# Attention with a Fourier mix and MLP: state products between the key and query turns, output turns behind the outputs, fixed PSUM banks, 17 unread products at the start

## The chip, the cores and the metric

The kernel runs on one core of one Trainium2 chip. The metric is the device time of an execution in microseconds; lower is better. A profile shows one execution: TensorE (PE, and PEld for its weight loads), VectorE (DVE), ScalarE (ACT), GpSimd (POOL) and the DMA queues, which SyncE (SP), ScalarE and GpSimd issue.

## The reference

```python
# batch 4, heads 8, seq 768, head_dim 64; blocks of 64 in the sequence
for b in range(nb):
    intra = einsum('bhic,bhjc->bhij', qb, kb) * Dmask      # lam**(i-j), lower triangle
    intra = einsum('bhij,bhjd->bhid', intra, vb)
    inter = einsum('bhid,bhde->bhie', qb * lam_pow, kv_state)
    out[:, :, sl] = intra + inter
    kv_state = lam_block * kv_state + einsum('bhsd,bhse->bhde', kb * rev_pow, vb)
# heads joined: x is (4, 768, 512)
mixed = real(fft(fft(x, axis=1), axis=2))
u = x + mixed
un = (u - mean(u)) / sqrt(var(u) + 1e-6)                   # over the 512 columns
out = u + maximum(un @ w_ch1, 0) @ w_ch2                   # 512 -> 2048 -> 512, weights come as float64
```

## The kernel before

All of it is float32. The attention works in chunks of 128 rows; a step `i` of twelve handles two chunks of one batch (three steps, `n = 0, 1, 2`, to a batch) for all eight heads, on 64x64 pieces of the array. A step has these parts, each a function:

- `turn_k` and `turn_q` turn keys and queries over by TensorE (eight 128x128 transposes each); ScalarE copies them from PSUM to `kT` and `qT` (lines 395, 401), and VectorE multiplies the queries by powers of lambda to `qs` (line 403);
- `scores` multiplies keys by queries into four PSUM banks (line 429), from which VectorE copies, times the decay, to `sc` (line 435, four instructions);
- `from_state` multiplies `qs` by the states of the chunks before (line 444), `within` the scores by v on top of that (line 450); ScalarE copies the result out as `oT`, in batch 0 also mirrored as `oTs` (lines 456 to 466);
- `to_state` multiplies scaled keys by v (line 409); VectorE adds it to a state (lines 417, 419) and GpSimd multiplies a state by its decay (`decayed`, line 424). `scale` scales the keys on GpSimd (line 389), after a small copy `scored` that waits for the first of VectorE's score copies; `sort` puts the keys of a later step in order (line 383);
- `back` turns the outputs over (`turned`, line 470) and copies them to rows, right half reversed (`put`, lines 480 and 481).

`attention` is a generator that calls these in an order written by hand, and every engine keeps that order. Where it yields, units of other work are put in: `w` is a third of a weight piece's conversion from float64 (`convert`: DVE and ScalarE, lines 264 to 273), `m` a step of the Fourier transform and normalisation of batch 0 (`fft_ln`, lines 601 to 839), `l` and `k` hidden-layer products (`mlp`, line 921). The lists `PLAN` (for each step a triple, one string for each yield) and `REST` (behind the attention) say how many. Behind them, from about 190 us on, a scheduler orders the rest by itself.

PSUM has eight banks, printed as `pa_96` to `pa_100` (banks 0 to 4) and `pm_101` to `pm_103` (banks 5 to 7). Turns, scores, output turns and at times state products draw in turn from banks 0 to 3 (`psum_t`), outputs from 4 and 5, Fourier products and most state products from 6 and 7 (`psum_a`).

Of the kernel before, what the change touches and what calls it, by code (L numbers as in the profile page):

```python
# [77 lines left out]
def kernel(  # L78
# [14 lines left out]
    C = 128  # L93
# [62 lines left out]
    turn = {"s": 0, "m": 0, "o": 0}  # L156
# [8 lines left out]
    def psum_t(shape):  # L165
        turn["s"] += 1
        return held_bank((turn["s"] - 1) % 4, shape)

    def psum_o(shape):
        turn["o"] += 1  # L170
        return held_bank(4 + (turn["o"] - 1) % 2, shape)
# [16 lines left out]
    make_identity(nc, ident)  # L188
    scan = nc.vector.tensor_tensor_scan
# [164 lines left out]
    po = {}  # L354
    mm = nc.tensor.matmul
# [35 lines left out]
    def turn_k(i):  # L391
        for r in range(2):
            pt = psum_t([128, HP, 128])
            lead(P(nc.tensor.transpose(pt[:, hp, :], k2[:, r, 128 * hp:128 * hp + 128], ident)) for hp in range(HP))  # L394
            P(nc.scalar.copy(kT[:, r], pt))

    def turn_q(i):
        for ch in range(2):
            pt = psum_t([128, HP, C])
# [5 lines left out]
    def to_state(i):  # L405
        n, vt, kd = i % SC, v_of[i % 2], k_of[i % 2]
        chunks = (0, 1) if n < SC - 1 else (0,)
        pu = [(psum_t if unread[0] or i < 2 else psum_a)([128, HP, D]) for _ in chunks]
# [3 lines left out]
        with tc.high_priority(100):  # L412
            for ch in chunks:
                c = 2 * n + ch
                s_new = states[(c + 1) % 3]
                if c == 0:
                    P(nc.vector.tensor_copy(s_new, pu[ch]))
# [9 lines left out]
    def scores(i):  # L427
        pss = [[psum_t([128, HP, C]) for _ in range(2)] for _ in range(2)]
# [11 lines left out]
    def from_state(i):  # L440
        n = i % SC
        po[i] = [psum_o([128, HP, C]) for _ in range(2)]
# [5 lines left out]
    def within(i):  # L448
# [4 lines left out]
        o = oT[i] = new(at, [128, HP, 2 * C], "oT")  # L453
        if b not in TURNED:
            for ch in range(2):
                P(nc.scalar.copy(o[:, :, C * ch:C * ch + C], po[i][ch]))
            return
        z = oTs[i] = new(at, [128, HP, 2 * C], "oTs", bufs=2)
        P(nc.scalar.copy(o[:, :, 0:C], po[i][0]))
        P(nc.scalar.copy(first if n == 0 else oTs[i - 1][:, :, 0:1], po[i][0][:, :, 0:1]))  # L460
        P(nc.scalar.copy(z[:, :, 2 * C - 1:C:-1], po[i][0][:, :, 1:C]))
        P(nc.scalar.copy(z[:, :, C:0:-1], po[i][1]))
        if n < SC - 1:
            P(nc.scalar.copy(o[:, :, C:2 * C], po[i][1]))
        else:
            P(nc.scalar.copy(z[:, :, 0:1], first))

    def turned(o, cols):
        px = psum_t([C, HP, 128])
# [3 lines left out]
    def put(px, x, n=128, crossed=False):  # L473
# [6 lines left out]
        P(nc.scalar.copy(x[0:n, 0:HM], px[0:n, 0:HM]))  # L480
        P(nc.scalar.copy(x[0:n, HM:DM], px[0:n, DM - 1:HM - 1:-1]))
# [1158 lines left out]
```

## Time and profile before

| | |
|---|---|
| median of 3 runs | 779.84 us (778.29 to 783.93) |
| the profiled execution | 780.86 us, its span 779.1 us |
| TensorE busy | 744.9 us (96%), 6872 instructions |
| VectorE busy | 604.6 us (78%) |
| ScalarE / GpSimd busy | 208.5 / 195.0 us |
| mean granted TensorE clock | 0.995 |

A line of the profile names the source line, the engine, the operation and `out<-in` with buffer numbers left out: `pa<-ident,w` is a transpose into a bank of the pool `pa`, whose source lies in a tile `w...`. TensorE's matmuls are pipelined and their ends are modelled, so its busy share says how seldom it has nothing in flight, not that it runs at its peak. A wait is put down to what came last; "issue" is time in which the engine waited for nothing that the profile shows.

### The profile page before, as it was taken

To read this page: it belongs to the slowest core of one execution; us is meant where nothing else is said; L and a number is where in the kernel's file an instruction comes from. 1 tells how busy PE (TensorE), PEld (TensorE's weight loads), DVE (VectorE), ACT (ScalarE), POOL (GpSimd) and SP (SyncE) were. 2 spreads that over 40 slices of the span, in tenths; PEclk is the share of its full clock that TensorE was granted. 3 is DMA by queue.
4 is the path that set the end of the run, shared out by engine and by line. 5 is a ranking of instruction groups with operands and counts; after the bars stand their busy time and mean duration, and the time that the engine had idled before them with its cause. 6 is when DMAs were issued, how large, how long until landed. Compare 5 with 4: busy or idle time off the path is not lost.

```text
span 779.1 us, 17084 instructions
## 1 busy us (share of the span) xinstructions
PE 744.9 (96%) x6872; PEld 644.2 (83%) x6872; DVE 604.6 (78%) x1163; ACT 208.5 (27%) x488; POOL 195.0 (25%) x221
## 2 busy tenths in 40 slices
PE   6998998799999989999999999999999999999997
PEld 5887887685486668659847889999999999999997
DVE  4578866668999788465965999689986699758984
ACT  2454545543141111002101221024311342024310
POOL 3344342210013214201104951260015000230013
PEclk9999999999999999999999999999999999999999
DMA  9879876535353447521341374775645455455452
GB/s 214 226 200 234 226 222 177 183 115 162 94 171 121 102 125 213 128 88 48 68 129 54 142 237 139 269 241 191 182 143 157 142 177 178 133 178 177 140 145 69
DMA packets 132740, 123.50 MB, mean 159 GB/s; under 512 B 67006, under 2 KB 93246, under 8 KB 132662
## 3 DMA queue, kind: packets, MB, share of 16 engines
q1 hardware_dynamic: 126902, 103.66, 46.6%
q0 software_dynamic: 4032, 12.99, 4.9%
q10 hardware_dynamic: 1728, 5.77, 2.3%
q8 instruction: 54, 0.88, 0.5%
q14 instruction: 24, 0.20, 0.1%
HBM read 90.66 MB, written 31.73 MB: 157 GB/s over the span
## 4 chain that ended last, share of the span: by engine, by line
PE 73%; DVE 9%; issue 7%; DMA 5%; POOL 3%; ACT 1%; SPq 0%; DVEq 0%; POOLq 0%; ACTq 0%
PE p L1370 21%; PE p L1296 17%; PE pm L935 7%; PE pm L921 7%; PE p L1203 5%; PE pa L921 2%; PE pa L429 2%; PE pa L727 2%; DMA words<-in_k_dram 1%; PE pa L450 1%; PE pa L400 1%; POOL fo L615 1%; PE pa L394 1%; PE pa L470 1%; DMA x<-xb,ix 1%
## 5 line engine op out<-in xcount | busy, mean ns | idle before, releaser
L935 PE MATMUL pm<-w,hr 128*128 128x512 f32 x240 | 106.5, 596 | 0.2 <-DVE w L273 0.2
L921 PE MATMUL pm<-ut,w 128*128 128x256 f32 x416 | 97.1, 386 | 3.3 <-ACT hr L929 2.4
L921 PEld LDWEIGHTS pm<-ut,w 128*128 128x128 f32 x416 | 78.4, 192 | 19.2 <-ACT hr L929 4.4
L935 PEld LDWEIGHTS pm<-w,hr 128*128 128x128 f32 x240 | 45.4, 191 | 51.7 <-issue 49.5
L1391 POOL TENSOR_TENSOR y<-y,u 128x512 f32<-128x512 f32 x12 | 19.9, 1660 | 186.8 <-DVE y L1400 155.5
L1370 PE MATMUL p<-tx,sx 128*128 128x128 f32 x400 | 52.7, 275 | 0.0
L1370 PEld LDWEIGHTS p<-tx,sx 128*128 128x128 f32 x400 | 48.6, 192 | 0.0
L1305 DVE TENSOR_TENSOR ha<-p,ha 128x512 f32<-128x512 f32 x60 | 40.0, 683 | 8.0 <-PE p L1296 7.9
L1376 ACT COPY y<-p 128x128 f32<-128x128 f32 x48 | 12.8, 266 | 103.6 <-PE p L1370 103.1
L1378 DVE TENSOR_TENSOR y<-p,y 128x128 f32<-128x128 f32 x92 | 25.4, 283 | 16.1 <-PE p L1370 9.4
L1370 PE MATMUL p<-w,ha 128*128 128x128 f32 x288 | 37.4, 275 | 0.0
L1305 DVE TENSOR_TENSOR hs<-p,hs 128x512 f32<-128x512 f32 x39 | 26.1, 683 | 12.7 <-PE p L1296 12.7
L929 ACT ACTIVATE hr<-pm 128x256 f32<-128x256 f32 x32 | 12.3, 383 | 86.8 <-PE pm L921 85.1
L1370 PEld LDWEIGHTS p<-w,ha 128*128 128x128 f32 x288 | 34.9, 192 | 0.1
L1296 PE MATMUL p<-sx,tx 128*128 128x128 f32 x264 | 33.9, 275 | 0.0
L429 PE MATMUL pa<-w 64*64 64x128 f32 x768 | 28.4, 284 | 5.2 <-issue 5.1
L615 POOL DMA_INDIRECT fo<-xa,ix x6 | 13.1, 2186 | 75.6 <-PE pa L727 69.9
L1296 PEld LDWEIGHTS p<-sx,tx 128*128 128x128 f32 x264 | 31.6, 192 | 0.0
L265 ACT ACTIVATE e<-e,cvt 128x512 uint16<-128x512 uint16 x32 | 22.9, 720 | 32.4 <-DVE e L264 32.2
L429 PEld LDWEIGHTS pa<-w 64*64 64x64 f32 x768 | 24.5, 140 | 7.8 <-issue 5.9
L910 POOL DMA_INDIRECT out_dram<-y,ix x12 | 13.7, 1143 | 66.5 <-DVE y L970 54.7
L1296 PE MATMUL p<-ur,w 128*128 128x128 f32 x216 | 28.0, 275 | 0.0
(338 smaller groups left out, 1926.5 us busy)
## 6 DMA issues: line engine op xcount, KB each, us to landing
tx<-td SPq DMA_DIRECT2D x84, 256.0 KB, 3.1
tx<-sd SPq DMA_DIRECT2D x63, 256.0 KB, 2.9
words<-in_moe_w_ch_dram SPq DMA_DIRECT2D x23, 512.0 KB, 3.4
w<-in_v_dram SPq DMA_DIRECT2D x12, 512.0 KB, 5.3
words<-in_k_dram SPq DMA_DIRECT2D x11, 512.0 KB
td<-tx SPq DMA_DIRECT2D x21, 256.0 KB, 2.0
raw<-in_moe_w_ch_dram ACTq DMA_DIRECT2D x9, 512.0 KB, 9.1
ud<-x SPq DMA_DIRECT2D x16, 256.0 KB, 2.4
```

The source lines that it names most:

```text
L265: P(nc.scalar.activation(pw, pw, AF.Relu, bias=cvt[:, 0:1], scale=8.0))
L429: lead(P(mm(pss[r][hi][HD[ch], hp, :], lhsT=kT[HD[hi], r, hp, D * ch:D * ch + D], rhs=qT[HD[hi], hp, C * ch:C * ch + C], start=True, stop= ...
L615: P(gather(out=eo[b][a][1][0:n, 1, 0:DM], out_offset=None, in_=xa[:, :], in_offset=row_of(a, n)))
L727: mm = P(nc.tensor.matmul(ps[:, n, :], lhsT=piece(a, i, n), rhs=cs[0:rows, a, i in (2, 3), n, :], start=(a == 0), stop=(a == 1)))
L921: P(nc.tensor.matmul(ps, lhsT=w1[:, c, 128 * fc:128 * fc + 128], rhs=ut[:, c, :], start=(c == 0), stop=(c == KO - 1)))
L935: return P(nc.tensor.matmul(ps, lhsT=hr[(fc - f0) // 4][:, fc % 4, 128 * i:128 * i + 128], rhs=w2[:, fc, :], start=(fc == f0), stop=(fc == ...
L1203: nc.tensor.matmul(ps, lhsT=s2.A[a][:, kt, 128 * i:128 * i + 128], rhs=U[b][:, kt, :], start=(first and kt == 0), stop=(kt == 1), skip_gro ...
L1296: nc.tensor.matmul(ps[:, 128 * i:128 * i + 128], lhsT=ab[m][0][:, 128 * i:128 * i + 128], rhs=ab[m][1], start=(start and i == 0), stop=Tru ...
L1305: V.tensor_tensor(o, p, o, op=ADD)
L1370: nc.tensor.matmul(ps[:, 0:HM // 2], lhsT=ab[m][0][i], rhs=ab[m][1][:, i, :], start=(start and i == 0), stop=(i == HF // 2 - 1), skip_grou ...
L1378: V.tensor_tensor(o, ps[:, 0:HM // 2], o, op=ADD)
L1391: nc.gpsimd.tensor_tensor(o, y, u, op=ADD)
```

## The change

The order in a step is now key turn, state products, sort, query turn, within, output turns, scores, from-state; it was key turn, query turn, output turns, state products, sort, within, scores, from-state. The banks have fixed roles: turns take 0 and 1, scores 0 to 3, outputs 4 and 5, and state products and output turns 6 and 7 with the Fourier products (2 and 3 while a Fourier product stands unread in PSUM). In batch 0 ScalarE copies outputs once, and `mirror` has VectorE make the mirrored tile from that copy, one step later. `put` is done by VectorE for even chunks of batch 0 and two mirrored ones, and the first state of a batch is copied by ScalarE. At the start 17 products of the identity matrix with itself, which nothing reads, stand ahead of the first turn. The normalisation of batch 0 is split in `scaled` and `turned_u`, with a tile of its own for each half. `PLAN` and `REST` are new: 18 units `w` instead of 19 in the attention, 38 instead of 41 in all, 48 `m` instead of 52 in the attention, and two `l` at its end.

```diff
+    for _ in range(17):
+        P(nc.tensor.matmul(banks[7][:, 0:128], lhsT=ident, rhs=ident, start=True, stop=True))
-    def psum_t(shape):
-        turn["s"] += 1
-        return held_bank((turn["s"] - 1) % 4, shape)
+    def spare_bank(shape):
+        if unread[0]:
+            turn["s"] += 1
+            return held_bank(2 + turn["s"] % 2, shape)
+        return psum_a(shape)
...
     def turn_k(i):
         for r in range(2):
-            pt = psum_t([128, HP, 128])
+            pt = held_bank(r, [128, HP, 128])
     def turn_q(i):
         for ch in range(2):
-            pt = psum_t([128, HP, C])
+            pt = held_bank(ch, [128, HP, C])
     def to_state(i):
-        pu = [(psum_t if unread[0] or i < 2 else psum_a)([128, HP, D]) for _ in chunks]
+        pu = [spare_bank([128, HP, D]) for _ in chunks]
...
                 if c == 0:
-                    P(nc.vector.tensor_copy(s_new, pu[ch]))
+                    P(nc.scalar.copy(s_new, pu[ch]))
     def scores(i):
-        pss = [[psum_t([128, HP, C]) for _ in range(2)] for _ in range(2)]
+        pss = [[held_bank(2 * r + hi, [128, HP, C]) for hi in range(2)] for r in range(2)]
...
+        for ch in range(2):
+            P(nc.scalar.copy(o[:, :, C * ch:C * ch + C], po[i][ch]))
+    def mirror(i):
+        if i // SC not in TURNED:
             return
+        n, o = i % SC, oT[i]
         z = oTs[i] = new(at, [128, HP, 2 * C], "oTs", bufs=2)
-        P(nc.scalar.copy(o[:, :, 0:C], po[i][0]))
-        P(nc.scalar.copy(first if n == 0 else oTs[i - 1][:, :, 0:1], po[i][0][:, :, 0:1]))
-        P(nc.scalar.copy(z[:, :, 2 * C - 1:C:-1], po[i][0][:, :, 1:C]))
-        P(nc.scalar.copy(z[:, :, C:0:-1], po[i][1]))
-        if n < SC - 1:
-            P(nc.scalar.copy(o[:, :, C:2 * C], po[i][1]))
-        else:
-            P(nc.scalar.copy(z[:, :, 0:1], first))
+        P(nc.vector.tensor_copy(first if n == 0 else oTs[i - 1][:, :, 0:1], o[:, :, 0:1]))
+        P(nc.vector.tensor_copy(z[:, :, 2 * C - 1:0:-1], o[:, :, 1:2 * C]))
+        if n == SC - 1:
+            P(nc.vector.tensor_copy(z[:, :, 0:1], first))
     def turned(o, cols):
-        px = psum_t([C, HP, 128])
+        px = spare_bank([C, HP, 128])
...
         for i in range(n):
+            if i:
+                mirror(i - 1)
             yield 3.0
             if i + 1 < n:
                 turn_k(i + 1)
-                turn_q(i + 1)
-            yield 2.0
-            if i:
-                back(i - 1)
+                to_state(i + 1)
+                if i + 2 < n:
+                    sort(i + 2)
+            yield 1.0
             if i + 1 < n:
-                to_state(i + 1)
-            if i + 2 < n:
-                sort(i + 2)
+                turn_q(i + 1)
             within(i)
...
-            yield 4.0
+            yield 5.0
+            if i:
+                back(i - 1)
             if i + 1 < n:
                 begin(i + 1)
...
-    REST = "lmwlmwlmwlmwwmkmwkmwkwwkwwlmwlmwlmwlwkmwkwkwkwwww"
+    REST = "wwwlwwwlmlmlmmmmlwlwmmkmkmkwkmmwkwwkwmmkwwwkwwww"
```

TensorE's queue in the step that prepares step 5 (batch 1): before, the two turns, the output turn and the state products stand in this order ahead of the products within the block.

```order
L394 MATMUL pa_98<-ident,w_147 128x128 x4
L394 MATMUL pa_99<-ident,w_147 128x128 x4
L400 MATMUL pa_96<-ident,w_147 128x128 x4
L400 MATMUL pa_97<-ident,w_147 128x128 x4
L470 MATMUL pa_98<-ident,oT_912 128x128 x4
L470 MATMUL pa_99<-ident,oT_912 128x128 x4
L409 MATMUL pm_102<-w_147,words_149 64x64 x16
L450 MATMUL pa_100<-w_146,w_147 64x128
```

The same place after the change (key turn now line 396, state products 411, query turn 402, within 452):

```order
L396 MATMUL pa_96<-ident,w_164 128x128 x4
L396 MATMUL pa_97<-ident,w_164 128x128 x4
L411 MATMUL pm_102<-w_164,words_166 64x64 x16
L402 MATMUL pa_96<-ident,w_164 128x128 x4
L402 MATMUL pa_97<-ident,w_164 128x128 x4
L452 MATMUL pa_100<-w_163,w_164 64x128
```

The state products moved ahead of the query turn, both turns share banks 0 and 1, and the output turn has gone behind the products within the block.

ScalarE's queue at the end of step 0 and the start of step 1, before: five output copies, three weight loads, an activation of a weight piece, then the key copies.

```order
L459 COPY oT_368<-pa_100 128x4x128
L460 COPY first<-pa_100 128x4
L461 COPY oTs_369<-pa_100 128x4x127
L462 COPY oTs_369<-pm_101 128x4x128
L464 COPY oT_368<-pm_101 128x4x128
L251 DMA raw_434<-in_moe_w_ch_dram 128x1024
L251 DMA raw_436<-in_moe_w_ch_dram 128x1024
L251 DMA raw_438<-in_moe_w_ch_dram 128x1024
L265 ACTIVATE e_440<-e_440,cvt 128x512
L395 COPY w_146<-pa_96 128x512
```

The same place after the change:

```order
L457 COPY oT_171<-pa_100 128x4x128
L457 COPY oT_171<-pm_101 128x4x128
L252 DMA raw_451<-in_moe_w_ch_dram 128x1024
L252 DMA raw_453<-in_moe_w_ch_dram 128x1024
L252 DMA raw_455<-in_moe_w_ch_dram 128x1024
L266 ACTIVATE e_457<-e_457,cvt 128x512
L397 COPY w_163<-pa_96 128x512
```

Three copies have left ScalarE, and the activation still stands ahead of the key copies.

TensorE's queue behind the last products within the block, before: the last output turn, hidden-layer products (921) and a turn of normalised rows (794).

```order
L450 MATMUL pm_101<-sc_153,w_147 64x128
L470 MATMUL pa_97<-ident,oT_2306 128x128 x4
L470 MATMUL pa_98<-ident,oT_2306 128x128 x4
L921 MATMUL pa_96<-ut_2082,w_146 128x256 x4
L921 MATMUL pa_97<-ut_2082,w_146 128x256 x4
L794 MATMUL pa_98<-ident,un_2337 128x128 x4
```

After (472 output turn, 864 turn of normalised rows, 741 to 746 a Fourier product, 939 hidden-layer products):

```order
L452 MATMUL pm_101<-sc_170,w_164 64x128
L864 MATMUL pm_103<-ident,e_2206 128x128 x4
L741 MATMUL pa_100<-dt,ys_175 128x128
...
L746 MATMUL pa_100<-dt,ys_176 128x128
L939 MATMUL pm_102<-ut_2202,w_163 128x256 x4
L939 MATMUL pm_103<-ut_2202,w_163 128x256 x4
L472 MATMUL pm_102<-ident,oT_171 128x128 x4
L472 MATMUL pm_103<-ident,oT_171 128x128 x4
```

Other products now stand between the last products within the block and the first of the remaining output turns.

More of the change, by code (lines that the diff above doesn't have):

```diff
@@ L354 @@
     po = {}
+    o_of = [new(at, [128, HP, 2 * C], "oT"), new(up, [128, KO, G * 128], "ut")]
     mm = nc.tensor.matmul
@@ L441, in from_state @@
         n = i % SC
-        po[i] = [psum_o([128, HP, C]) for _ in range(2)]
+        po[i] = [held_bank(4 + ch, [128, HP, C]) for ch in range(2)]
         chunks = (0, 1) if n else (1,)
@@ L492, in back @@
                     px = turned(oT[i], cols)
[L493 to L497 removed]
+                    put(px, x, copy=nc.vector.tensor_copy if ch == 0 else None)
                 continue
@@ L851, in one, with scaled, turned_u @@
                 return 1.0
+            def scaled(g):
+                sh, rs = chains.pop(g)
+                uts[b, g] = new(up, [128, KO, G * 128], "ut")
+                uns[g] = []
+                for i in range(G):
+                    un = new(ep, [128, DM], "e") if i else new(np_, [128, DM], "un", bufs=1)
+                    u = xs[b, TT[g][i]]
+                    for o, x in ((un[:, 0:HM], u[:, 0:HM]), (un[:, HM:DM], u[:, DM - 1:HM - 1:-1])):
+                        P(nc.scalar.activation(o, x, AF.Identity, bias=sh[:, i:i + 1], scale=rs[:, i:i + 1]))
+                    uns[g].append(un)
+                    yield 1.0
+            def turned_u(g, i):
+                pt = psum_a([128, KO, 128])
+                lead(P(nc.tensor.transpose(pt[:, c, :], uns[g][i][:, 128 * c:128 * c + 128], ident)) for c in range(KO))
+                P(nc.scalar.copy(uts[b, g][:, :, 128 * i:128 * i + 128], pt))
+            uns = {}
             s = summed(1, *wide(1))
@@ L872, in fft_ln @@
             yield one(s)
-            yield one(n2)
-            yield one(n2)
+            yield from scaled(2)
+            for i in range(G):
+                turned_u(2, i)
+                yield 1.0
             yield one(s)
-            yield one(n2)
-            yield one(n2)
             stats(0)
             yield 1.0
-            for _ in range(4):
-                yield one(n0)
+            yield from scaled(0)
+            for i in range(G):
+                turned_u(0, i)
+                yield 1.0
             return
```

54 lines of the change are left out of this document (21 added, 33 removed).

## The prediction

> **What bounds the kernel now.** I read the page from the top: who is busy, and when.
>
> ```profile
> PE 744.9 (96%) x6872; PEld 644.2 (83%) x6872; DVE 604.6 (78%) x1163; ACT 208.5 (27%) x488; POOL 195.0 (25%) x221
> ...
> PE   6998998799999989999999999999999999999997
> ```
>
> TensorE is busy for 96% of the span, nearly everywhere. Of its 40 slices (19.5 us each) six are under 9, and four of these lie in the first eight, the attention that the change rewrites. A table by stage says what stands beside it there.
>
> ```profile
> 0.00:20.00 20.00, 13.96 (x257) 11.63 (x260) 10.08 (x29) 5.68 (x9) 7.07 (x15) 1.00 1.02 210
> ...
> 40.00:60.00 20.00, 18.37 (x489) 16.27 (x487) 16.05 (x29) 11.11 (x29) 10.36 (x16) 1.00 0.79 205
> 60.00:80.00 20.00, 17.79 (x451) 16.08 (x450) 16.67 (x33) 8.76 (x23) 9.10 (x9) 1.00 0.96 233
> ...
> 160.00:180.00 20.00, 20.00 (x97) 17.59 (x96) 11.11 (x21) 10.40 (x22) 0.36 (x2) 0.99 0.25 79
> 180.00:200.00 20.00, 19.75 (x56) 10.32 (x55) 19.69 (x40) 5.36 (x9) 0.00 (x0) 1.00 0.51 158
> ```
>
> The columns after the stretch are its length, then TensorE, weight loads, VectorE, ScalarE and GpSimd (busy us and instructions), granted clock, DMA share and GB/s. In the first three rows the DMA engines are 0.79 to 1.02 busy and VectorE has up to 16.67 of 20 us: TensorE leads, but two others stand close behind. From 160 us on TensorE has its 20 of 20. The work that it does is the same after the change (17 products apart), so the change can give no more than TensorE's idle time before 160 us. The list of waits, for TensorE in the first 157 us (total, times, longest):
>
> ```profile
> PE pa L394 <- DMA w<-in_k_dram: 5.1, 1, 5.1
> PE pa L429 <- issue: 5.1, 5, 1.8
> PE pa L470 <- ACT oT L456: 2.8, 1, 2.8
> PE pa L470 <- ACT w L395: 1.4, 1, 1.4
> PE pa L470 <- DVE w L403: 1.4, 2, 1.1
> PE pm L794 <- ACT un L785: 1.1, 1, 1.1
> PE pa L409 <- DVE w L403: 0.8, 2, 0.6
> PE pm L444 <- DVE st L417: 0.8, 1, 0.8
> PE pm L921 <- ACT ut L798: 0.7, 1, 0.7
> ```
>
> The first row is the arrival of k, which nothing moves. The other rows shown make 14.1 us: that is what is to be had, beside what TensorE loses inside groups that run slowly. The profiled run took 780.86 us (span 779.1 and 1.8 around it), 1.0 above the median of 779.84. I work out a difference from the profiled run and take it off the median.
>
> **The start: 17 products.**
>
> ```profile
> 1.01 0.29 POOL masks.py:199 TENSOR_SCALAR_AFFINE_SELECT ident<-ident 128x128 f32<-128x128 f32 x1
> 5.12 2.22 PE L394 MATMUL pa<-ident,w 128*128 128x128 f32 x8 [5.12 <-DMA w<-in_k_dram]
> 9.53 4.21 PE L429 MATMUL pa<-w 64*64 64x128 f32 x62
> 54.70 1.93 PE L429 MATMUL pa<-w 64*64 64x128 f32 x64
> 101.07 0.88 PE pa L394 x8
> ```
>
> The first turns take 2.22 us where the same eight take 0.88 later, and the first scores 4.21 where they take 1.93: TensorE starts at about half speed. 32 score products are 64 instructions, so 17 products are 34. Between 0.88/8 = 0.11 us and 2.22/8 = 0.28 us each, they take 3.7 to 9.4 us from 1.30 us on, when the identity matrix is ready; I take 6.7 (early ones slow, late ones fast). They end near 8.0, and the turn of k waits for them instead of its data: 2.9 us late. It wins 2.3 on the scores and 2.6 on 16 turns, but turn of q now shares the banks of turn of k and waits for ScalarE's copies. I book 0; the ends are -2.3 (scores alone) and +2.9 (delay alone).
>
> By the Trainium skill's page "TensorE: Matmul & The Clock Gate" (Part 4: PE-mode transpose), transposes do not count as work for the clock gate, and by its Part 1 full clock needs a busy window of about 3.4 us. The trace agrees so far: the scores that follow 16 transposes are still slow. By that page alone the products should pay, which is the last rival below.
>
> **One step of batch 1**, from the chain of waits (start, us, what):
>
> ```profile
> 57.69 1.16 PE pa L394 x8
> 58.85 1.20 PE pa L400 x8
> ...
> 63.96 0.66 issue
> 64.62 1.86 PE pa L429 x59
> ...
> 67.46 1.06 PE pa L394 x8
> ```
>
> The step is 9.77 us: key turn (L394), query turn (L400), output turn (L470), state products (L409), products within the block (L450, hidden by the chain's small pieces), scores (L429), products from the state (L444).
>
> *Fetch stalls.* In the scores TensorE stops without a wait on anything (0.66 here, 5.1 us in five). Around the longest:
>
> ```profile
> q8 instruction: 1, 0.02, 4.4%
> 73.50 0.49 PE L429 MATMUL pa<-w 64*64 64x128 f32 x9
> 75.50 0.34 PE L429 MATMUL pa<-w 64*64 64x128 f32 x4 [1.51 <-issue]
> ```
>
> The first line is the DMA queue of instructions from 73.0 to 74.3 us: one packet, just ahead of the resumption. So I read these stalls as waits for instructions. State, within, scores and from-state products now run in one piece, 64+64+64+32 instructions with their weight loads, in about 5.5 us. The new order puts a turn of eight slow instructions between each two of them. I book -4.0 of the 5.1; ends 0 and -5.1.
>
> *Fixed banks.* The key turn now writes banks 0 and 1, which VectorE frees first; output turns and state products take 6 and 7. The rows L470, L409 and L444 behind DVE make 1.4+0.8+0.8 = 3.0 us. In batch 0 the output turn has four groups on two banks, and the third waits for a put, so 1.0 stays: -2.0; ends 0 and -3.0. The turns at 1.16 and 1.20 against 0.88 lose 0.6 a step, to banks still being read as I take it. Some three to four steps' worth should go, -2.0; ends 0 and 11 x 0.6 = -6.6.
>
> *Turn k behind ScalarE.*
>
> ```profile
> 27.53 0.72 ACT L265 ACTIVATE e<-e,cvt 128x512 uint16<-128x512 uint16 x1 [3.89 <-DVE e L264]
> ```
>
> The 1.4 us at L470 <- ACT L395 come from this instruction, which waits for a weight's DMA ahead of the key copies. It stands at the same place in ScalarE's queue after the change; now the query turn waits behind it. 0; ends -1.4 and +1.5.
>
> *The new wait.* State products now follow the key turn at once, and they need the keys that GpSimd scales.
>
> ```profile
> 54.73 1.16 DVE L601 TENSOR_TENSOR fe<-fo,x 65x512 f32<-65x512 f32 x1
> 56.86 0.68 DVE L435 TENSOR_TENSOR w<-pa,decay 128x512 f32<-128x512 f32 x1
> 57.67 0.19 POOL L542 COPY scored<-w 128x1 f32<-128x1 f32 x1 [2.33 <-DVE w L435]
> 57.81 1.92 POOL L389 TENSOR_TENSOR words<-words,decay 128x1024 f32<-128x1024 f32 x1
> 59.69 2.00 POOL L424 TENSOR_TENSOR st<-st,qpow 128x256 f32<-128x256 f32 x1
> ```
>
> GpSimd starts when VectorE's first score copy is done (56.86 + 0.68) and ends at 59.73. The key turn ends at 58.85: 0.9 us of waiting that the query and output turns hide today. That VectorE copy was itself late: the first half of the scores, begun at 54.70, is done after 1.93/2, at 55.7, and VectorE was in folds until 56.86. On time the wait would be near nothing. I take 0.45 us in the seven steps without Fourier products ahead of the key turn: +3.0; ends 0 and 11 steps x 1.1 = +12. Behind the waiting state products stand the query turn, the products within and the next scores, so each microsecond is TensorE's.
>
> *The copies.* ScalarE loses three of its five output copies per step of batch 0, VectorE gets a mirrored one of 1020 elements. With puts of even chunks and without four state copies VectorE gets some 5 us more, before 60 us, where it has 10 to 16 of 20. It runs behind the score copies while TensorE turns keys: 0, and up to +5 if VectorE has no room.
>
> The Trainium skill's page "SBUF — State Buffer" (Who interferes with whom) speaks against it: a VectorE copy within SBUF, or a sum of two SBUF tensors, shares ports with GpSimd, and one blocks the other. The trace shows the like: GpSimd's 128x256 product took 2.00 us beside VectorE's folds. By the page each of three mirrored copies could cost GpSimd its own length, an estimate of some 1.3 us each from 0.68 for 512 elements, +4 in the sum.
>
> *The end.* The waits at L470 <- ACT oT (2.8), L794 (1.1) and L921 (0.7) stand after the last step. Now hidden-layer products stand between, output turns come in pairs with products ahead, and both normalised tiles are scaled before their turns: -4.5 of 4.6; end 0. Loads now go out ahead of the stores of the output turn on SyncE's queue, and nothing waits for those stores before 160 us.
>
> *Sum:* 0 - 4.0 - 2.0 - 2.0 + 0 + 3.0 + 0 - 4.5 = **-9.5 us**, so 771.4 for the profiled run and **770.3** at the median. Behind 160 us it carries through: one weight piece less is converted by the end of the list, but VectorE has 9 us free from 160 to 180 and the new list puts conversions first.
>
> **The rivals.** (1) VectorE becomes the bound from 58 to 100 us. For: 16.67 of 20 us there, and the new list packs 21 fold units into two steps that had 15. Against: it is not full in any slice before 160. At its present load a step cannot go under 9.77 x 16.67/20 = 8.1 us; with denser folds and in-order waits I put four steps 0.8 us later and 3 us at the weights from 180 us, where it has 19.69 of 20: 776.5. (2) The fetch stalls stay, being bound to DMA load and not to order: 774.3. (3) Slower: the state products wait in every step for GpSimd, since VectorE's score copy comes behind puts and folds. At 1.55 us (0.45 and the lateness of 1.1) in 11 steps it costs 17 in place of 3: 784.3. It decides from (9.5 + 3.0)/11 = 1.1 us a step. (4) The start pays as the clock rule has it, with the scores' 2.3 us won and no delay: 768.0.
>
> **Chances.** Forecast 0.48, (1) 0.18, (2) 0.12, (3) 0.10, (4) 0.12. The range for 8 in 10 is 762 to 781: below, rival (4) with all the waits of the list gone; above, rival (1) with the bounds of the new wait. About 1% (7.8 us, 772.0) is what a measurement here can tell from no change. The forecast lies on the faster side by little, so half of (1)'s and nearly all of (2)'s chance is same: faster 0.52, same 0.37, slower 0.11.
>
> **What would show it.** Right: state products that wait for GpSimd under 0.6 us, fewer idle pieces put down to issue, no wait of 2.8 us near 140, and the last products within the block ending 5 us or more before 142 us. Wrong: VectorE at 18 of 20 between 60 and 100 us; state products idle over a microsecond in each step; a first key turn after 8 us with slow scores behind it; or TensorE with new idle time between 160 and 240 us, which would mean that VectorE's weights did not follow.

## The result, and the profile after

The changed kernel takes 784.55 us (median of 20 runs, 782.36 to 789.43) against 779.0 us before (20 runs): ratio 1.0079, 95% interval 1.0061 to 1.0096. It is slower by 5.5 us where -9.5 was forecast, and outside the range. Its profiled execution took 782.43 us (span 780.7), that of before 780.86 (779.1): less apart than the medians, because before's profiled execution lies 2 us above its median and this one 2 below.

The page after, its busy line and its TensorE slices:

```profile
PE 748.1 (96%) x6906; PEld 645.8 (83%) x6906; DVE 607.5 (78%) x1174; ACT 206.1 (26%) x475; POOL 202.5 (26%) x221
...
PE   8899999899999799999999999999999999999996
```

TensorE is busy 3.2 us more than before; the 17 products, from 1.35 us on for 6.05, are more than that, since the first turns now run fast. The table by stage (length, TensorE, weight loads, VectorE, ScalarE, GpSimd, clock, DMA share, GB/s):

```profile
0.00:20.00 20.00, 16.10 (x290) 14.56 (x294) 9.26 (x28) 5.63 (x10) 7.69 (x16) 1.00 0.97 209
40.00:60.00 20.00, 18.50 (x463) 16.23 (x452) 13.85 (x28) 8.54 (x20) 9.04 (x15) 1.00 0.69 176
60.00:80.00 20.00, 18.09 (x460) 15.88 (x449) 17.65 (x33) 9.02 (x22) 7.66 (x9) 1.00 0.72 166
160.00:180.00 20.00, 18.57 (x96) 15.95 (x95) 10.53 (x23) 10.92 (x24) 2.86 (x4) 1.00 0.25 84
180.00:200.00 20.00, 19.69 (x54) 9.83 (x53) 19.63 (x39) 5.92 (x11) 0.00 (x0) 1.00 0.63 193
```

VectorE reaches 17.65 of 20 us at 60 to 80, one of the signs that the forecast named for its first rival, and TensorE is no longer full at 160 to 180 us (18.57 where it had 20.00). TensorE's waits in the first 157 us:

```profile
PE pm L411 <- POOL words L391: 1.9, 5, 0.9
PE pa L431 <- issue: 1.8, 2, 0.9
PE pm L189 <- POOL ident masks.py:199: 1.4, 1, 1.4
PE pm L452 <- issue: 1.3, 1, 1.3
PE pm L939 <- DVE w L274: 1.3, 1, 1.3
PE pm L741 <- DVE st L421: 1.1, 1, 1.1
...
PE pm L411 <- DMA w<-in_v_dram: 0.9, 1, 0.9
PE pa L431 <- DVE w L405: 0.8, 1, 0.8
```

The row of 2.8 us at the last output turns is gone, the new row of state products on GpSimd (first) is there at 1.9, and smaller rows have taken the place of those removed. The first scores start at 9.85 us (9.53 before), the first hidden-layer products at 143.63 (146.12 before). That is 2.5 us ahead. But two output turns, which stood ahead of that point, now stand behind it (from 147.08 and 148.65 us on) and take 2.1 us; all other products up to there are the same. So only some 0.4 us is won there. Three places show where the rest of the forecast went.

**Passages between turns and products.** TensorE in one step of batch 1, before and after (start, us, line):

```profile
78.05 1.09 PE L394 MATMUL pa<-ident,w 128*128 128x128 f32 x8
78.98 1.04 PE L400 MATMUL pa<-ident,w 128*128 128x128 f32 x8
79.85 1.04 PE L470 MATMUL pa<-ident,oT 128*128 128x128 f32 x8
80.82 1.46 PE L409 MATMUL pm<-w,words 64*64 64x64 f32 x59
```

```profile
80.17 1.09 PE L396 MATMUL pa<-ident,w 128*128 128x128 f32 x8
81.49 1.16 PE L411 MATMUL pm<-w,words 64*64 64x64 f32 x64 [0.22 <-ACT w L397]
82.58 1.09 PE L402 MATMUL pa<-ident,w 128*128 128x128 f32 x8
```

Read the column 128*128 or 64*64, the part of the array that is used, and the starts. Query turn to output turn takes 0.87 us; output turn to state products 0.97. In the trace a turn starts 0.109 us after a turn, a product on 64x64 pieces 0.202 after a turn, a turn 0.149 to 0.200 after such a product, and product after product 0.04 to 0.09. The old order has two passages in a step, the new one six. Over the attention the trace has 31 before and 67 after; at about 0.1 us beyond the interval without a passage that is some 3 and 7 us. A Fourier product (65*128) is not split into pieces, and a turn follows it after 0.163, its own pace: the passage costs where the split of the array changes. The Trainium skill's page "TensorEngine Tiling (Array Packing)" (Tiling Modes, Key Properties) says that a change of tiling mode drains the TensorE; the trace agrees, with about 0.1 us each way. The forecast had no term for it.

**The end.** GpSimd's two last scatters of outputs, before and after, and behind each pair how long they took to land (last number; a stretch of the DMA view):

```profile
769.54 0.98 POOL L910 DMA_INDIRECT out_dram<-y,ix  x1 [5.50 <-DVE y L1378]
773.08 0.97 POOL L910 DMA_INDIRECT out_dram<-y,ix  x1 [2.56 <-DVE y L1378]
```

```profile
out_dram<-y,ix POOLq DMA_INDIRECT x2, 2.8
```

```profile
769.19 0.98 POOL L928 DMA_INDIRECT out_dram<-y,ix  x1 [5.50 <-DVE y L1396]
774.66 0.97 POOL L928 DMA_INDIRECT out_dram<-y,ix  x1 [4.48 <-DVE y L1396]
```

```profile
q8 instruction: 1, 0.02, 1.7%
...
out_dram<-y,ix POOLq DMA_INDIRECT x2, 4.7
```

The last scatter comes 5.47 us behind the one ahead of it, where it was 3.54: in both it is issued 0.76 us after that one has landed, and beside the slower landing lies a packet of instructions (770.7 to 772.4). The span ends 7.0 us after the start of TensorE's last product where it was 5.1. The page counts 55 such packets of 16 KB after and 54 before.

**The weights.** Behind the attention VectorE stands still for 6.6 us, and ScalarE shows why (VectorE's row, then ScalarE's):

```profile
151.19 0.74 DVE L273 SCALAR_TENSOR_TENSOR e<-raw,e 128x512 uint16<-128x512 uint16 x1 [6.56 <-ACT e L266]
```

```profile
147.76 0.37 ACT L483 COPY x<-pm 128x256 f32<-128x256 f32 x1
...
150.43 0.73 ACT L266 ACTIVATE e<-e,cvt 128x512 uint16<-128x512 uint16 x1
```

The exponents (L266) stand in ScalarE's queue behind the last output copies. From 143 to 184 us VectorE finishes 7 weights where it finished 8 (that line's instructions alone, after and before):

```profile
143.00:184.00 41.00, 4.37 (x7) 1.00 0.45 154
```

```profile
143.00:184.00 41.00, 5.51 (x8) 0.96 0.45 154
```

The same weight stays 3.2 us later than before until 240 us, and near 258 us TensorE stops for VectorE:

```profile
PE pm L939 <- DVE x L984: 3.6, 1, 3.6
```

Such a stop costs more than its length. In all traces here the granted clock is 1.00 or 0.50. Behind the start and up to the last products each stretch at 0.50 lasts 3.4 us or two or four times that, and in the 3.4 us ahead of each TensorE was idle for 1.5 us or more. Here one begins at 261.5 us; at half clock 3.4 us lose 1.7 us of work, as an estimate. The kernel before has its like: it stops at 277 us for 2.9 us (17.23 of 20 us busy), and a stretch at half clock follows (0.91 in the mean).

```profile
260.00:280.00 20.00, 17.23 (x52) 9.56 (x51) 12.91 (x31) 2.46 (x6) 3.23 (x4) 1.00 0.39 74
280.00:300.00 20.00, 19.88 (x99) 17.22 (x100) 17.52 (x41) 4.27 (x13) 7.29 (x11) 0.91 0.62 214
```

Counted where both kernels have done the same products, the changed one is 0.3 us behind at 249 us and 1.3 behind at 300. A wait of 1.8 us for VectorE at 507 us in the kernel before is not there, and its last product starts 0.3 us ahead (773.67 against 774.02). With 1.9 for the end that makes 1.6 us, the difference of the two spans. The other 3.9 of the 5.5 us are not located: one execution against another does not show them.

### The profile page after: what moved, and what is told of

It reads as the page before. It is cut to its first block, busy times and chain, and to the rows that moved or that the text cites. A ratio compares the mean times of both kernels' runs of the same rounds, so it can differ in the third digit from the quotient of the medians.

```text
span 780.7 us, 17132 instructions
## 1 busy us (share of the span) xinstructions
PE 748.1 (96%) x6906; PEld 645.8 (83%) x6906; DVE 607.5 (78%) x1174; ACT 206.1 (26%) x475; POOL 202.5 (26%) x221
## 5 line engine op out<-in xcount | busy, mean ns | idle before, releaser
L939 PE MATMUL pm<-ut,w 128*128 128x256 f32 x456 | 106.2, 384 | 7.8 <-DVE x L984 3.6
L939 PEld LDWEIGHTS pm<-ut,w 128*128 128x128 f32 x456 | 85.6, 192 | 24.6 <-issue 6.8
L947 ACT ACTIVATE hr<-pm 128x256 f32<-128x256 f32 x37 | 14.1, 381 | 99.7 <-PE pm L939 99.7
L266 ACT ACTIVATE e<-e,cvt 128x512 uint16<-128x512 uint16 x32 | 23.0, 721 | 41.3 <-DVE e L265 40.0
L617 POOL DMA_INDIRECT fo<-xa,ix x6 | 17.4, 2905 | 61.5 <-DVE e L265 57.4
L431 PE MATMUL pa<-w 64*64 64x128 f32 x768 | 25.0, 273 | 2.8 <-issue 1.8
L437 DVE TENSOR_TENSOR w<-pa,decay 128x512 f32<-128x512 f32 x24 | 16.4, 685 | 14.3 <-PE pa L431 14.3
```

Source lines behind the costliest of these rows:

```text
L266: P(nc.scalar.activation(pw, pw, AF.Relu, bias=cvt[:, 0:1], scale=8.0))
L431: lead(P(mm(pss[r][hi][HD[ch], hp, :], lhsT=kT[HD[hi], r, hp, D * ch:D * ch + D], rhs=qT[HD[hi], hp, C * ch:C * ch + C], start=True, stop= ...
L437: P(nc.vector.tensor_tensor(sc[hi][:, r], pss[r][hi], decay[:, hi::2, 1 - r:1 - r + C], op=ALU.mult))
L617: P(gather(out=eo[b][a][1][0:n, 1, 0:DM], out_offset=None, in_=xa[:, :], in_offset=row_of(a, n)))
L939: P(nc.tensor.matmul(ps, lhsT=w1[:, c, 128 * fc:128 * fc + 128], rhs=ut[:, c, :], start=(c == 0), stop=(c == KO - 1)))
L947: P(nc.scalar.activation(t, ps, AF.Relu))
```

## The experiments

Each kernel was timed beside the kernel before on the same chip. In rows that begin with "before +" the edit is made to the kernel before, in the others to the changed kernel.

| edit | median us | ratio to before, 95% | mean clock |
|---|---|---|---|
| before, unchanged | 780.4 | 1.0005 (0.9986 to 1.0025) | 0.992 |
| before + 17 products | 783.75 | 1.0070 (1.0053 to 1.0087) | 0.992 |
| before + 17 products of one column | 786.78 | 1.0086 (1.0056 to 1.0116) | 0.991 |
| before + 34 products of one column | 792.25 | 1.0141 (1.0091 to 1.0191) | 0.991 |
| before + fixed banks | 778.14 | 0.9995 (0.9971 to 1.0019) | 0.993 |
| before + copies on VectorE | 783.85 | 1.0059 (1.0032 to 1.0085) | 0.989 |
| before + banks, copies, products | 784.48 | 1.0087 (1.0066 to 1.0108) | 0.994 |
| before + one unit ahead of the last outputs | 777.08 | 0.9967 (0.9943 to 0.9991) | 0.995 |
| before + two units | 775.72 | 0.9938 (0.9917 to 0.9959) | 0.996 |
| before + two units and banks | 778.81 | 0.9984 (0.9956 to 1.0012) | 0.993 |
| changed | 784.55 | 1.0079 (1.0061 to 1.0096) | 0.993 |
| without products | 784.24 | 1.0082 (1.0053 to 1.0112) | 0.993 |
| copies on ScalarE | 787.54 | 1.0109 (1.0092 to 1.0126) | 0.990 |
| without products, copies on ScalarE | 787.03 | 1.0094 (1.0069 to 1.0118) | 0.992 |
| without the wait of `scale` | 786.42 | 1.0103 (1.0079 to 1.0128) | 0.994 |
| three turns together | 785.75 | 1.0096 (1.0080 to 1.0112) | 0.993 |
| two turns together | 782.49 | 1.0062 (1.0039 to 1.0086) | 0.995 |
| two turns together, without products | 783.84 | 1.0045 (1.0013 to 1.0076) | 0.994 |
| without products, one unit moved back | 785.89 | 1.0075 (1.0047 to 1.0104) | 0.992 |

The last column matters for a few rows: within one kernel the span rises by some 0.65 us for each 0.001 that the mean granted clock is lower (fitted over the runs of these kernels; 0.62 to 0.72 by which are counted). The runs of before beside them have 0.991 to 0.994.

### The kernel before, unchanged

> The kernel before, unchanged, timed as a kernel of its own. The profiled runs differ by 1.6 us (782.43 after, 780.86 before), the medians by 5.5 (784.55 against 779.0). Theory C (the granted clock): the runs of the changed kernel show a mean clock of 0.986 to 0.996, 0.9925 on the average; if the clock makes the rest of the difference, the runs here stay at 0.995 or more. Rival: the same spread of clocks here, and then the difference of the medians comes from waits that the one profile does not show. Time 779.0, ratio 1.000 within 0.002.

Its clock spreads as widely as that of the changed kernel (0.986 to 0.998, mean 0.992). Theory C falls: the clock doesn't make the 5.5 us. Its profiled execution, the one with 0.986, shows what a low mean is. Behind the stop at 277 us the half clock lasts 13.6 us instead of 3.4, and TensorE does 70 products from 280 to 300 us where it did 99:

```profile
280.00:300.00 20.00, 19.16 (x70) 16.66 (x71) 14.07 (x34) 3.35 (x9) 5.58 (x9) 0.66 0.42 148
```

### The products

```diff
-    for _ in range(17):
-        P(nc.tensor.matmul(banks[7][:, 0:128], lhsT=ident, rhs=ident, start=True, stop=True))
```

Taken out of the changed kernel:

> The changed kernel without the 17 products at first, nothing else changed. Theory F (fetches): the page of the changed kernel counts one packet of 16 KB more on the queue of instructions than the program needs with 68 fewer TensorE instructions, and that packet lies at 770.6 to 772.3 us, beside the next to last scatter of the outputs, which lands after 4.7 us where it landed after 2.8; the last scatter waits for it, and the time from the last product to the end is 7.0 us where it was 5.1. Without the products the packet lies behind the end again: 5.1 us there. The start: first scores at 9.5 in place of 9.9. In all 782.3. Rival (clock): the products pay by a faster start, and without them the first scores end 2 us later, time 784 to 786, with the end still 7.0 us behind the last product.

Put into the kernel before, at the same place:

> The kernel before with the 17 products at first, nothing else changed. Theory F: the same packet now lies beside the last scatters of this kernel too, the end comes 6.5 to 7 us after the last product in place of 5.1, and the first scores start 0.3 us later; time 780.5 to 781.3 against 779.0. Rival (clock): the time falls by 1 to 2 us, to 777.5, since the first scores run in 1.9 us in place of 4.2.

The end is as theory F says, both ways: 54 packets and 3.53 us between the last scatters without the products, 55 packets and 5.51 with them in the kernel before. All kernels here with 54 packets have 3.53 or 3.54, those with 55 have 4.8 to 5.6, but for one, below. The start of the kernel with products did win: its first scores took 2.5 us (4.2 before) and the second ones began at 20.7 us instead of 21.3. But the gain was gone at the third (32.7 and 32.5). Fast first scores are not the products' alone: in the executions of three kernels without them (banks alone; two units; two turns together) they took 2.6 to 2.7 us. Waits on nothing in the attention rose as well, from 5.7 (4.4 in the run above) to 7.7:

```profile
PE pa L431 <- issue: 4.3, 4, 1.7
PE pm L452 <- issue: 1.8, 2, 1.0
PE pa L452 <- issue: 0.7, 1, 0.7
PE pa L411 <- issue: 0.6, 1, 0.6
PE pm L446 <- issue: 0.3, 1, 0.3
```

In the changed kernel without the products hardly any are left:

```profile
PE pm L409 <- issue: 0.6, 2, 0.4
...
PE pa L400 <- issue: 0.2, 1, 0.2
```

In the profile of the kernel before with the products a stretch at half clock follows the wait for the last outputs (2.86 us, then 3.4 at 0.50 from 145.6 us on); without them the wait is as long (2.85) and no such stretch follows. So the products cost the kernel before 5.4 us, more than was expected. Taking them out of the changed kernel won nothing that the runs can tell (784.24, ratio 1.0082), though 4 us of waits on instructions and 1.9 at its end went. Its state products now waited 1.9 us for a load of v and 2.1 for GpSimd, and two stretches at half clock (from 31.3 and 120.1 us on) stand in this attention, none in that of the changed kernel's profile. Whether the 5.4 us come from the place of the fetches or from the products' time was put to two more runs, with `rhs=ident[:, 0:1]`:

> The kernel before with 17 products of one column in place of the 17 of 128 columns: the same 68 more TensorE instructions, but they end before the first keys arrive at 5.1 us, and the start stays slow as it was. The kernel before with the 17 full products took 783.75 against 778.4. Theory F (place of the fetches): the 16 KB packets of instructions come at other places of the program, the end 7.0 us behind the last product, more waits on nothing in the attention (7 to 8 us in place of 4.4 and 5.7): time 781 to 784. Rival (the start): the loss comes from the products' own time and the faster first scores that run into the loads; then 780.5, the 1.9 us of the end alone.

> The same with 34 products of one column, 136 more instructions, 3.5 us of TensorE's last stage once more. Theory F: the last packet comes 3 to 4 us earlier than with 17, at 768 us, ahead of the next to last scatter, and the end comes back to 5 to 5.5 us behind the last product, though the program is longer; the waits on nothing in the attention take a third value. Time 779 to 782, below that with 17. Rival (the start, or the number of instructions): time as with 17 or longer.

They don't decide it, since a product of one column was no shorter: 34 instructions took 7.4 us, each starting 0.21 us after the other, as their weight loads do, and the first scores came at 12.2 and 19.4 us in place of 9.5. Nor do they make the start fast: the first turns still took 1.95 us, where they take 1.04 behind the products of 128 columns. The waits on instructions were 5.2 and 6.2 us, not the 7 to 8 of theory F. The attention behind them took 137.0 us both times (136.6 before), so a late start is passed on whole. One part holds: with 34 the packet lies 6 us ahead of the last product and the scatters are 3.53 us apart again, though there are 55 packets. What counts is that a fetch falls beside that scatter, not the number of instructions.

### The order of the turns

```diff
                 turn_k(i + 1)
+                turn_q(i + 1)
+            if i:
+                back(i - 1)
+            yield 1.0
+            if i + 1 < n:
                 to_state(i + 1)
```

(query turn in banks 2 and 3, state products in 0 and 1, where output turns go too while a Fourier product stands unread; the same calls further behind are taken out)

> The changed kernel with the key, query and output turns of a step in one run again, and the state products behind them; banks, copies, list of fill-in work and 17 first products stay. Theory S (passages): in the trace a product that follows a turn starts 0.202 us after it where a turn follows a turn after 0.109, and a turn that follows products starts after 0.149 or 0.200 where products follow products after 0.04 to 0.09. The change has six such passages in a step where the kernel before has two, 0.41 us a step, 4.9 us in twelve. With two again the stretch from the first scores to the first hidden-layer products falls from 133.8 us to about 127 (4.9 for the passages and 1.9 for the waits of state products on GpSimd, which the query and output turns hide again), and the time to 778 if it carries through, 781 if VectorE's weights keep their place. Rival W (banks): waits for banks come back and the stretch stays within 1 us of 133.8, time 784. Rival V (VectorE): the stretch falls but the time does not, 784, since VectorE's weights set the end.

The passages fell to 31, as theory S says, and the intervals of 0.202 between turns with them. The time did not fall. Products in one long run wait for instructions, and the turns of outputs for the copies that empty their bank:

```profile
PE pm L472 <- DVE x L484: 3.8, 2, 2.5
PE pm L452 <- issue: 3.6, 2, 2.0
PE pa L431 <- issue: 3.3, 3, 1.3
```

Only key and query turn together (45 passages; banks as in the run above), with the products and without:

```diff
                 turn_k(i + 1)
+                turn_q(i + 1)
                 to_state(i + 1)
...
             yield 1.0
-            if i + 1 < n:
-                turn_q(i + 1)
             within(i)
```

> The changed kernel with key and query turns together, the state products behind both (in banks 0 and 1), the output turns where the change put them: four passages between turns and products a step in place of six. Theory S: 0.2 us a step less, 2.4 us in all, and no wait of the state products for GpSimd (1.9 us): the stretch from the first scores to the first hidden-layer products 129.5 to 131 in place of 133.8, time 781 to 782.5. Rival (fetches): products in longer runs wait more for instructions (4.9 us of waits on nothing in the changed kernel, 8.2 with all turns together), and the time stays at 784 to 786.

> The changed kernel without the 17 products, and with key and query turns together (four passages a step in place of six). If what the runs showed adds up: the end 5.0 us behind the last product, 2.3 us less for the passages, waits on nothing of 1 to 3 us, no waits for GpSimd: the stretch from the first scores to the first hidden-layer products 130 to 132 in place of 134.9 without the products, time 779 to 781. Rival: fewer passages give as much back in waits on banks and copies, and the time stays at 782 to 784.

The first is 1.3 us faster than the changed kernel by the ratios (2.1 by the medians), the second 2.9 (0.4) faster than the changed kernel without products; the intervals overlap in both. The stretch that theory S would shorten took 133.9 and 134.7 us, no less than the 133.8 of the changed kernel; the second waits 5.9 us on instructions. So that passages cost the whole what their intervals add up to is not shown: the orders that save them have other waits instead.

### GpSimd's scaling

```diff
-                P(nc.gpsimd.tensor_copy(scored, sc[0][:, 0, 0, 0:1]))
```

> The changed kernel without the small copy by which GpSimd waits for VectorE's first score copy before it scales the next keys. If the five waits of state products on GpSimd (1.9 us in all) are what they seem, they go, and the time falls by 0 to 1.9 us, to 782.6 to 784.5. Rival: GpSimd now works beside the score copies and both grow (the scaling from 1.92 us, the copies from 0.68), and the time is the same or up to 3 us longer.

The wait on GpSimd fell to 0.5 us, but the time did not fall (786.42), and the state products waited for their other operand instead:

```profile
PE pm L411 <- DMA w<-in_v_dram: 3.5, 2, 2.2
```

### The copies

In the changed kernel all mirrored and output copies go back to ScalarE, the mirrored ones still from the first copy and one step later:

```diff
-        P(nc.vector.tensor_copy(z[:, :, 2 * C - 1:0:-1], o[:, :, 1:2 * C]))
+        P(nc.scalar.copy(z[:, :, 2 * C - 1:0:-1], o[:, :, 1:2 * C]))
...
-                    put(px, x, copy=nc.vector.tensor_copy if ch == 0 else None)
+                    put(px, x)
```

> The changed kernel with the mirrored copies and all output copies on ScalarE, as before the change. Rival V (VectorE): VectorE has some 5 us less to do before 142 us, its weights, which come 3.2 us later than before the change from 183 us on, come 3 us earlier, and the time falls to 781. Theory S: VectorE does not set the pace before 142 us, ScalarE's output copies come later instead, and the time stays at 784.5 within 1.5.

Rival V falls: the time rose by 3.0 us, of which the lower clock (0.990) would make 2. The same without the products:

> The changed kernel without the 17 products and with all copies on ScalarE: what is left of the change is the order, the banks and the list of fill-in work. If the costs measured on the kernel before add up (products 4 to 5 us, copies 2 to 4.6), 784.5 falls to 776 to 778, and order and list cost nothing. Rival O (order): the key turn's copies now stand right ahead of the state products and query turn, and behind output copies in ScalarE's queue (4.4 us of waits of the query turn on ScalarE's key copies in the run with these copies); the order itself costs 4 to 5 us, and the time is 783 to 786.

```profile
PE pa L400 <- ACT w L395: 4.6, 3, 3.3
```

The costs do not add up, and the time is even above rival O's range. In the new order the query turn uses the banks of the key turn, and with all copies on ScalarE it waits for ScalarE's key copies, as rival O says. Order and list of fill-in work were not tried apart. On the kernel before, the copies alone (`mirror`, `put` and the two fixed output tiles as in the change, nothing else):

```diff
+            if i:
+                mirror(i - 1)
...
-                        put(px, x)
+                    put(px, x, copy=nc.vector.tensor_copy if ch == 0 else None)
```

> The kernel before with the mirrored copies and the output copies of even chunks on VectorE alone. The forecast's term: 0. Rival V: VectorE has 5 us more before 142 us, its score copies and folds come later, and the time rises by 1 to 3 us, to 780 to 782, with the weights from 183 us on 1 to 2 us later.

4.6 us slower, of which the lower clock of these runs (0.989) would make 2. VectorE is busy 40.9 us instead of 37.1 in the first 60, and the output turns wait longer, for its query products (L404) and ScalarE's key copies (L396):

```profile
PE pa L471 <- ACT w L396: 3.3, 3, 1.4
PE pa L471 <- DVE w L404: 2.2, 2, 1.9
```

### The banks

On the kernel before:

```diff
-            pt = psum_t([128, HP, 128])
+            pt = held_bank(r, [128, HP, 128])
...
-            pt = psum_t([128, HP, C])
+            pt = held_bank(2 + ch, [128, HP, C])
...
-        pu = [(psum_t if unread[0] or i < 2 else psum_a)([128, HP, D]) for _ in chunks]
+        pu = [held_bank(ch, [128, HP, D]) for ch in chunks]
```

> The kernel before with the fixed banks alone (key turn 0 and 1, query turn 2 and 3, state products 0 and 1, scores 0 to 3, output turns in the two others), copies on ScalarE as before, order and list as before, no products at first. The forecast's term: -2.0 (waits behind VectorE at the output turns, state products and products from the state go): 777. Rival B: a fixed bank waits for its one reader where the rotation took the next that was free, and the stretch from the first scores to the first hidden-layer products grows by 1 to 2 us over 136.6: 780 to 781.

Not the banks alone: output turns also stand ahead of the second string of fill-in work, the mirrored copies come from the first copy and a step later, and the first state of a batch and one put of VectorE's go to ScalarE. No difference that the runs can tell: 0.9995. Rival B's longer stretch did not come (132.7 us in the profile). With the copies and the products added, on the old order and list:

> The kernel before, order and list of fill-in work included, with the fixed banks, the copies on VectorE and the 17 products alone. If banks and copies bring what the forecast booked (2 us and nothing), the time is 779.0 - 2 + 2 for the 17 products, 779 within 1. Rival V (the copies burden VectorE): its weights come 2 to 3 us later than in the kernel before from 183 us on, and the time is 782 to 784. If the list of fill-in work is what makes the weights late, they stand where they stood.

784.48, as slow as the whole change; its weights stood 1.7 us later than in the kernel before, near what rival V said.

### The end of the attention

Two hidden-layer units `l` of the list `REST` move into the attention's last string; with one unit, only one does:

```diff
-            ("mw", "w", "mm"), ("mm", "m", "mmm"), ("mw", "mmmw", "mm")]
-    REST = "lmwlmwlmwlmwwmk...
+            ("mw", "w", "mm"), ("mm", "m", "mmm"), ("mw", "mmmw", "mmll")]
+    REST = "mwmwlmwlmwwmk...
```

> The kernel before with two hidden-layer units moved ahead of the last output turns. The wait of 2.9 us at 142 us goes, TensorE is 2.9 us ahead near 150 us. If it carries through: 776.5. Theory V: the output copies come 0.6 us later, ScalarE's exponents and VectorE's weights stay where they are or come later, TensorE waits for VectorE near 277 us as much longer, and the time stays at 779 or rises to 781.

> The same with one unit of 1.7 us. If it carries through: 777.7, the wait at 142 us 1.2 in place of 2.9. Theory V: 779 to 780.

Both are faster, in order of the wait that they fill. Before, and with two units:

```profile
145.14 1.14 PE L470 MATMUL pa<-ident,oT 128*128 128x128 f32 x8 [2.85 <-ACT oT L456]
```

```profile
143.34 3.72 PE L921 MATMUL pm<-ut,w 128*128 128x256 f32 x16
146.90 1.04 PE L470 MATMUL pa<-ident,oT 128*128 128x128 f32 x8
```

The wait is gone and the time falls by 3.0 us in medians (4.8 by the ratio of the runs; a higher clock in these runs could make 2 of it). Theory V falls here: the weights from 183 us on come 1.7 us earlier, with one unit 3.2, and what was won ahead of them carried through. 775.72 us (six runs) is the lowest median of the study, below both. In the changed kernel, which has this part already, one unit moved behind the outputs again, without the products:

```diff
-            ("mww", "", "mww"), ("mm", "", "mw"), ("mmww", "mm", "mmmll")]
-    REST = "wwwlwwwl...
+            ("mww", "", "mww"), ("mm", "", "mw"), ("mmww", "mm", "mmml")]
+    REST = "lwwwlwwwl...
```

> The changed kernel without the 17 products, and with one of the two hidden-layer units that stand ahead of the last output turns behind them. Theory V (weights): ScalarE's exponents of the next weight, which wait in its queue behind the last output copies (VectorE stands idle for 6.6 us there), come 1.7 us earlier, VectorE's weights from 183 us on 1.5 us earlier, and the stall of 3.8 us near 258 us falls to about 2; TensorE waits 1 us more for the last outputs. Time 783 against 784.2. Rival: VectorE is held up elsewhere (5.9 us near 163 us), its weights stay where they are, and the time rises by 1 us.

It won nothing: the stall near 260 us was still 3.6 us. But its state products waited 3.7 us for v in the profile, and its weights came 1.7 us later than without the move, so the test is weak. The idle time behind ScalarE's copies is not what makes the weights late, or not alone. The two units and the banks on the kernel before, both edits as above (the banks with what goes with them):

> The kernel before with the two parts of the change that cost nothing: the fixed banks, and two hidden-layer units ahead of the last output turns; order, copies and start as before. If they add: -0.5 and -3.5 to -4.8 on 779: 774 to 775. Rival: in the trace of the banks alone the wait for the last outputs is down to 1.1 us already, so that the units bring only 1 to 1.5 us beyond the banks: 776.5 to 777.5.

The interval holds 1: its runs lie between 773 and 786 us. Beside the banks the gain of the units is not seen again, so that its 3 us stand on the two runs above alone.

## Why the prediction was wrong, step by step

- **The start (booked 0).** The mechanism was told rightly (products, a later first turn, faster scores), but the sum ended at the first scores. On the kernel before the products cost 5.4 us. 1.9 of it is at the end of the program, where no term looked. Waits on instructions in the attention are 2 to 3 us more, and one wait more is followed by half clock. Taken out of the changed kernel they gave nothing back, so how much of its 5.5 us is theirs stays open. The rival by the clock rule has its faster scores, 2.5 us instead of 4.2; they were lost within two steps. In the faster scores the trace agrees with the Trainium skill's page "TensorE: Matmul & The Clock Gate" (Part 1); what they bring to the whole no rule there says.
- **Fetch stalls (booked -4.0).** The cause was read rightly: in the profiles before and after, ten of the eleven such waits of 0.3 us or more end 1.2 to 1.7 us behind a 16 KB packet of instructions. Without products the new order waits 0.8, 1.8 and 2.2 us on nothing in three kernels, the old one 4.4 and 5.7 in two executions of the kernel before. But the changed kernel's own profile has 4.9 us (2.1 and 2.9 in two more kernels with products), so hardly any of the 4.0 came.
- **Slow turns (booked -2.0).** This step failed. The durations 1.16 and 1.20 came from one step; of the eleven key turns only two were slow. And the turns became dearer: a turn between two products pays two passages. By the intervals the new order pays some 3.6 us for 36 more of them, the largest term missing from the sum, though no run that saved them won it back whole.
- **Fixed banks (booked -2.0).** With the small changes beside them 0.9995, that is -0.4 us with -2.3 to +1.5, so the booked size is not excluded. In that profile the output turns wait for ScalarE in place of VectorE.
- **The new wait (booked +3.0).** 1.9 us in five waits, so the size was right and rival (3) did not come. But the state products also need v earlier: 0.9 us in the changed kernel, 3.5 where the wait for GpSimd was cut to 0.5, and 1.9 and 3.7 in two kernels without products.
- **The copies (booked 0, up to +5).** The upper end was the right one on the old order: +4.6, at least 2 of it not the clock's. VectorE at 17.65 of 20 us was the cover that the text doubted. GpSimd's state product took 1.05 and 1.14 us where it ran beside a mirrored copy, 0.62 and 0.81 at the same places without. A copy of four elements that ran beside GpSimd's scaling took 0.51 us and ended with it, 0.16 where nothing ran beside it. So the trace agrees with the Trainium skill's page "SBUF — State Buffer" (Who interferes with whom) that the two block each other, but it shows some 0.4 us a time, not the estimated 1.3, and not the whole 4.6.
- **The end waits (booked -4.5).** Half right: the 2.8 us went, and this part alone made the kernel before some 3 us faster. But 3.4 us of other waits stand behind the attention now, for ScalarE (0.7 at L864, 1.4 at L939) and for VectorE's weights (1.3 at L939).
- **The carry-through (assumed whole).** This step failed too in the changed kernel, where weights came 3.2 us later and 3.6 us of waiting appeared near 258 us, though for two units on the kernel before it held. The prediction's "From 160 us on TensorE has its 20 of 20" was a misreading: the kernel before has 17.23 of 20 at 260 to 280, with a stop for VectorE (table above). Whether order, copies or list delay the weights stays open.

The costs don't add. Products, copies and order each make a slow kernel alone (783.8, 783.9, and 787.0 with only order, list and banks), and together, at 784.5, they are no slower. In an attention where TensorE, the copies, the loads and the fetches run within a few tenths of each other, what one part frees another takes. That this is the reason is argued from the rows that move between the runs; no run shows it by itself, and where 3.9 of the 5.5 us lie is not known.

## What to carry to other kernels

Count the passages between whole-array turns and products on pieces of the array before splitting a run of turns: here each takes 0.1 us, and 36 more some 3.6 by the trace. Look at what follows a wait of TensorE of 1.5 us or more: a stretch at half clock can cost as much again. A few instructions more on the busiest engine move every later fetch of instructions, so look at what lies beside a fetch at the end of the program, where nothing hides it. And test the parts of a change alone: the one that won some 3 us here was a place in a list, hidden under the rest of the change.

## What the runs showed of the hardware

Three things were not expected. A 16 KB fetch for TensorE, for which TensorE itself did not wait, delayed an indirect scatter from 2.8 to 4.7 us, and with it the end of the kernel. Products of one column took 0.21 us each at the start, as long as those of 128 before the clock rose, and their weight loads start at the same distance. And the mean granted clock of one kernel on one core spread from 0.986 to 0.998 between executions, worth 8 us. It counts the stretches at half clock, of 3.4 us or two or four times that, behind waits of TensorE; the same wait of 2.9 us had one behind it in one kernel and none in another. With 5 to 12 runs of a kernel the 95% intervals here reach 0.17 to 0.5% to either side.
